# Block order for every batch, a carry-over of FFN work, earlier first transposes and fewer constants in an attention-then-FFN kernel

## The chip, the cores and the metric

The kernel runs on one core of a Trainium2 chip. The metric is device time in microseconds (us), lower is better. Executions of one kernel mostly agree within about one per cent. Now and then a run falls into a slow state; such runs are left out of every comparison.

The engines are called as in the profile: PE is TensorE (matmuls), PEld its weight loads, DVE is VectorE, ACT is ScalarE, POOL is GpSimd (here causal masks and the issuing of loads), SP issues the stores. Each engine has its own list of instructions, and one that takes long holds up those behind it on its engine.

## The reference, cut to what matters

```python
# q, k, v: (4 batches, 8 heads, 768 tokens, 64); chunks of 32 keys, 24 chunks a head
ub     = sum_d max(q * k_min[chunk], q * k_max[chunk])      # bound of each (query, chunk)
ub     = where(chunk is not in the future, ub, -1e9)
top    = the 6 chunks of largest ub, per query
scores = q @ k.T / 8, only where the key's chunk is in top and key <= query
attn   = softmax(scores) @ v
x      = attn, heads side by side                           # 3072 tokens x 512
out    = relu(x @ w_in) ** 2 @ w_out                        # 512 -> 2048 -> 512
```

## The kernel before

All matmuls are in bf16. Heads go in pairs, four pairs a batch; queries go in two blocks of 384 per batch, so there are eight query blocks. Four kinds of work share the engines.

A *preparation* of a pair transposes k and q on PE, reduces k to chunk maxima and minima on DVE, multiplies for the bounds `ub`, finds the sixth largest bound per query, and transposes the resulting selection into extra rows of q. This is a chain that goes PE, DVE, PE, DVE, ACT many times. All its results on the matmul side use one buffer, the tag `tp` of pool `pst`, so each step waits until the one before was read:

```python
pst = ctx.enter_context(tc.tile_pool(name="pst", bufs=1, space=PSUM))   # tag "tp"
psf = ctx.enter_context(tc.tile_pool(name="psf", bufs=2, space=PSUM))   # tag "ff"
...
for nm in ("k", "q"):
    pt = pst.tile([128, nt, HT, 128], BF16, tag="tp", name=nm + "T")
    ...                                              # 6 or 12 transposes by PE
    by_token = pt.rearrange("d t j p -> d t p j")
    if nm == "q":
        for hh in range(2):
            nc.scalar.copy(qs[s][hh][0:D, cols]..., by_token[...])       # ACT
        continue
    kt = work.tile([128, QB * nt], BF16, tag="kt", name="kt")
    nc.vector.tensor_copy(kt..., by_token)                               # DVE
    ...                                              # kr: max and min per chunk
```

The *attention* of a pair and a block is `ps` (scores, PE), `e` (exponential, ACT), a causal mask (POOL), `av` (values, PE), `rc` (one over the sum, ACT) and `xT` (the normalized result, DVE). A batch's first block has 3 key tiles and its second block has 6.

The *FFN* of a block can start when all four pairs of that block have written `xT`. It is cut into 28 units of four matmuls: 16 `ph` units (up) and 12 `py` units (down). A pacer puts units between the score matmuls. It drops what it could not place: the last line throws a debt away.

```python
def run_ffn(cols):
    pace["due"] += cols * pace["rate"]
    while pace["due"] >= 1.0 and ffn:
        ffn.pop(0)()
        pace["due"] -= 1.0
    pace["due"] = min(pace["due"], 1.0)
```

The *order of work*: batches 0 and 3 do their first block for all pairs and then their second (block order), batches 1 and 2 do both blocks of one pair and then the next pair (pair order). In pair order both blocks of a batch become ready for the FFN only near the batch's end.

```python
Bk = [(p, blk) for blk in range(NBLK) for p in range(NP)]
for b in range(1, B):
    heads = range(NP * b, NP * (b + 1))
    if b < B - 1:
        Bk += [(p, blk) for p in heads for blk in range(NBLK)]
    else:
        Bk += [(p, blk) for blk in range(NBLK) for p in heads]
```

At the start, 12 tiles get the same constant rows by ACT, and DVE sets the constants of all six buffer sets and two large fields of ones before its first real work.

The softmax here doesn't subtract the row's maximum and nothing guards it: scores larger than these inputs give would overflow.

## Time and profile before

The time is 357.2 us, the median of three runs (356.99 to 359.16). The profiled execution, one more run of 359.0 us, has a span of 357.3 us from its first to its last instruction. Two lines of its page, first the engines' busy times and then what all DMAs moved:

```profile
PE 308.7 (86%) x2096; PEld 160.0 (45%) x2096; DVE 218.6 (61%) x678; ACT 253.3 (71%) x589; POOL 96.7 (27%) x243
...
DMA packets 48158, 20.30 MB, mean 57 GB/s; under 512 B 41984, under 2 KB 44032, under 8 KB 48128
```

PE is the busiest engine, but an average of 86% hides different stages. The view by windows shows them. I cut the span at the last write to `xT` of batch 0's first block (48.2 us), of batch 0, 1, 2 and 3, and leave what follows as the tail. A row has the window, its length, then busy time and instructions of each engine, the granted PE clock as a share of full speed, the DMA share and GB/s:

```profile
core 0: us, PE busy (x) PEld busy (x) DVE busy (x) ACT busy (x) POOL busy (x), PEclk, DMA share, GB/s
0.00:48.20 48.20, 24.27 (x155) 11.04 (x155) 37.40 (x131) 29.04 (x60) 29.92 (x59) 1.00 1.37 172
48.20:101.90 53.70, 48.39 (x359) 25.06 (x358) 40.02 (x136) 41.52 (x102) 17.34 (x43) 0.98 0.65 68
101.90:173.20 71.30, 64.77 (x466) 34.41 (x464) 49.69 (x144) 55.87 (x135) 23.27 (x57) 0.89 0.46 49
173.20:246.70 73.50, 68.92 (x515) 36.63 (x512) 48.29 (x145) 57.75 (x136) 14.59 (x45) 1.00 0.06 23
246.70:311.50 64.80, 60.19 (x392) 31.77 (x392) 31.77 (x92) 50.14 (x123) 11.58 (x41) 1.00 0.06 21
311.50:357.30 45.80, 42.20 (x220) 21.06 (x218) 11.47 (x32) 19.01 (x38) 0.00 (x0) 0.99 0.11 41
```

The reader should see three stages: a start in which PE is busy half of the time and DVE is the fullest engine (37.4 of 48.2 us), a middle with PE nearly full, and a tail of 45.8 us that is FFN alone. The chain that ended last, read at its end (start, duration, work, count), shows the tail as matmuls nearly back to back:

```profile
310.60 0.65 PE ph L256 x4
...
311.27 10.53 PE ph L256 x60
321.80 10.36 PE py L270 x48
...
332.83 10.53 PE ph L256 x60
343.36 10.37 PE py L270 x48
```

Here four up matmuls take 0.65 us, 162 ns each, and 48 down matmuls take 10.36 us, 216 ns each. (All 64 up matmuls from 310.60 to 321.80 us average 175 ns, because a short hole follows every second unit. The prediction below divided the 10.53 us of 60 matmuls by 64 and so writes 164.) The Trainium skill, "TensorE: Matmul & The Clock Gate", section "Back-to-back issue gap", gives N/2.4 + 2.5 ns for N columns as the gap of an isolated matmul when the array is warm. This is 162.5 and 215.8 ns for 384 and 512 columns, and the trace agrees. So the tail can hardly be shortened but by having less work in it. One FFN unit of four matmuls costs about 0.77 us on average there (16 of 0.70 us and 12 of 0.86 us).

The middle has a hole that the window rows hide. The timeline of ACT, cut to the rows of the FFN (`ob` copies a finished output out, `ht` is the relu of an up result; start, duration, what), shows that in batch 1 the FFN stood still for 20 us:

```profile
140.90 0.58 ACT L275 COPY ob<-py 128x512 f32<-128x512 f32 x1
...
161.58 0.87 ACT L261 ACTIVATE ht<-ph 128x384 bf16<-128x384 f32 x2 [0.62 <-PE ph L256]
```

Both FFN blocks of batch 0 were done by 141 us, and pair order had no new block ready until 161 us. I counted FFN units per segment from the number of `ph` and `py` matmuls in each window: 1.5, 28, 39, 53, 48 and, in the tail, 55. Batch 1 has the fewest although it is as long as batch 2.

DVE's first real work, behind memsets, is this row of its timeline:

```profile
10.96 0.56 DVE L183 COPY kt<-kT 128x384 bf16<-128x384 bf16 x1
```

### The profile page before, as it was taken

The page shows a single profiled execution, that of the slowest core. Times are in us where ns is not written, and L with a number is a line of the kernel's source. Part 1 is how long each engine was busy: PE and PEld are TensorE (multiplying, and loading weights), DVE is VectorE, ACT ScalarE, POOL GpSimd, SP SyncE. Part 2 cuts the span into 40 slices and gives each one's busy share as a digit, 9 for nine tenths or more (in the row PEclk, how much of TensorE's full clock was granted, in tenths as well). Part 3 has the DMA queues.
Part 4 walks back from the last instruction along what each step waited for, and adds up shares of the span by engine and source line. Part 5 has one row for each costly group of instructions (what it writes and reads, how often), then busy time and mean ns, then how long its engine had stood idle before and what let it go on. Part 6 is the DMA issues. An engine that isn't in the chain of part 4 may idle for free.

```text
span 357.3 us, 6146 instructions
## 1 busy us (share of the span) xinstructions
PE 308.7 (86%) x2096; PEld 160.0 (45%) x2096; DVE 218.6 (61%) x678; ACT 253.3 (71%) x589; POOL 96.7 (27%) x243
## 2 busy tenths in 40 slices
PE   0276689999789998789999999999799999999996
PEld 0132345444345544445544554455444555454542
DVE  7688779747958766769482868379991331250320
ACT  6665568955968865977957897778749996671541
POOL 8275642222451332218221212212013111000000
PEclk9999999999969999959999999999999999999999
DMA  8999990190490039009400000100000000101102
GB/s 88 177 198 183 204 153 3 11 195 32 57 62 2 1 52 206 9 2 60 30 31 31 29 2 0 61 30 3 0 31 30 29 2 29 55 7 42 48 2 86
DMA packets 48158, 20.30 MB, mean 57 GB/s; under 512 B 41984, under 2 KB 44032, under 8 KB 48128
## 3 DMA queue, kind: packets, MB, share of 16 engines
q0 software_dynamic: 44672, 13.63, 36.0%
q1 hardware_dynamic: 3456, 6.29, 4.7%
q8 instruction: 16, 0.26, 0.3%
q14 instruction: 14, 0.11, 0.1%
HBM read 27.26 MB, written 6.29 MB: 94 GB/s over the span
## 4 chain that ended last, share of the span: by engine, by line
PE 57%; ACT 20%; DVE 17%; issue 4%; POOL 1%; ACTq 0%; POOLq 0%; DVEq 0%
PE ph L256 19%; PE py L270 16%; PE ps L346 7%; ACT e L350 5%; ACT rc L328 4%; ACT kqc L121 2%; ACT qsc L177 2%; PE kT L170 2%; ACT rc L331 2%; DVE qp L209 2%; DVE kr L187 2%; ACT ht L261 2%; DVE xT L334 2%; PE qT L170 2%; DVE kt L183 2%
## 5 line engine op out<-in xcount | busy, mean ns | idle before, releaser
L350 ACT ACTIVATE e<-ps 128x384 bf16<-128x384 f32 (+2 forms) x288 | 110.8, 425 | 36.8 <-PE ps L346 28.8
L256 PE MATMUL ph<-xT,w_in_sb 128*128 128x384 bf16 x512 | 108.9, 332 | 4.3 <-ACT ht L261 3.8
L353 POOL TENSOR_SCALAR_AFFINE_SELECT e<-e 128x128 bf16<-128x128 bf16 x192 | 58.7, 320 | 172.5 <-ACT e L350 171.6
L346 PE MATMUL ps<-qsc,kqc 88*128 88x384 bf16 (+2 forms) x288 | 80.7, 314 | 7.9 <-ACT e L350 4.7
L261 ACT ACTIVATE ht<-ph 128x384 bf16<-128x384 f32 x128 | 62.8, 494 | 15.9 <-PE ph L256 12.5
L256 PEld LDWEIGHTS <-w_in_sb 128*128 128x128 bf16 x512 | 49.0, 99 | 37.0 <-issue 11.2
L314 PEld LDWEIGHTS <-vo 128*128 128x128 bf16 x288 | 28.2, 103 | 29.9 <-DVE xT L334 7.5
L346 PEld LDWEIGHTS <-kqc 88*128 88x128 bf16 x288 | 28.2, 102 | 22.7 <-issue 8.3
L275 ACT COPY ob<-py 128x512 f32<-128x512 f32 x24 | 14.1, 585 | 27.5 <-PE py L270 27.5
L187 DVE TENSOR_REDUCE kr<-kt 128x24 bf16<-128x768 bf16 (+1 forms) x40 | 29.9, 786 | 0.5
L177 ACT COPY qsc<-qT 64x768 bf16<-64x768 bf16 (+1 forms) x40 | 26.6, 666 | 3.0 <-PE qT L170 2.1
L92 POOL DMA_DIRECT2D vo<-in_v_dram x24 | 21.4, 896 | 14.8 <-PE av_2351 L314 8.7
L183 DVE COPY kt<-kT 128x768 bf16<-128x768 bf16 (+1 forms) x20 | 15.9, 797 | 11.6 <-PE kT L170 11.1
L240 DVE COPY qsc<-sT 24x640 bf16<-24x640 bf16 (+2 forms) x40 | 16.7, 417 | 8.5 <-PE sT L235 8.0
L216 PE MATMUL ub<-kbd,qp 128*128 128x48 bf16 x80 | 9.8, 190 | 12.8 <-DVE qp L209 12.1
L170 PE MATMUL qT<-ident,qn 128*64 128x128 bf16 x192 | 10.8, 245 | 7.5 <-DVE kt L183 7.3
L331 ACT ACTIVATE rc<-rc 128x384 f32<-128x384 f32 x32 | 16.5, 516 | 0.2
L170 PE MATMUL kT<-ident,kn 128*64 128x128 bf16 x192 | 12.5, 247 | 4.4 <-DMA kn<-in_k_dram 4.4
L216 PEld LDWEIGHTS <-qp 128*128 128x128 bf16 x80 | 6.1, 98 | 22.3 <-DVE qp L209 22.2
L170 PEld LDWEIGHTS <-kn 128*64 128x64 bf16 x192 | 7.4, 120 | 17.7 <-issue 7.3
L211 DVE TENSOR_SCALAR qm<-qsc 64x640 bf16<-64x640 bf16 (+2 forms) x40 | 14.1, 352 | 0.0
L170 PEld LDWEIGHTS <-qn 128*64 128x64 bf16 x192 | 7.3, 120 | 14.5 <-issue 13.7
(644 smaller groups left out, 504.3 us busy)
## 6 DMA issues: line engine op xcount, KB each, us to landing
out_dram<-ob SPq DMA_DIRECT2D x24, 256.0 KB, 2.0
vo<-in_v_dram POOLq DMA_DIRECT2D x24, 128.0 KB, 4.4
kn<-in_k_dram POOLq DMA_DIRECT2D x3, 768.0 KB, 8.7
qn<-in_q_dram POOLq DMA_DIRECT2D x3, 768.0 KB, 11.3
w_in_sb<-in_moe_w_in_dram POOLq DMA_DIRECT2D x2, 1024.0 KB, 12.4
w_out_sb<-in_moe_w_out_dram POOLq DMA_DIRECT2D x2, 1024.0 KB, 12.3
kn<-in_k_dram POOLq DMA_DIRECT2D x1, 384.0 KB, 15.8
qn<-in_q_dram POOLq DMA_DIRECT2D x1, 384.0 KB, 10.1
```

Of the source, the lines that this page charges most:

```text
L170: nc.tensor.matmul(pt[D * hh:D * hh + D, t, j], lhsT=n[:, 2 * (2 * hp + hh) + n0 + t, j], rhs=ident, is_transpose=True, start=True, stop=True)
L177: nc.scalar.copy(qs[s][hh][0:D, cols].rearrange("d (t p j) -> d t p j", t=nt, j=HT), by_token[D * hh:D * hh + D])
L183: nc.vector.tensor_copy(kt.rearrange("d (t p j) -> d t p j", t=nt, j=HT), by_token)
L187: nc.vector.tensor_reduce(kr[:, m], kt.rearrange("d (c j) -> d c j", j=CH), axis=AX.X, op=op)
L256: nc.tensor.matmul(ph, lhsT=w_in_sb[:, ki, 128 * f:128 * (f + 1)], rhs=xT[:, ki, t0:t0 + QB], start=(ki == 0), stop=(ki == NKI - 1))
L261: nc.scalar.activation(ht, ph, ACT.Relu)
L270: nc.tensor.matmul(py, lhsT=h2[f][:, 128 * t:128 * (t + 1)], rhs=w_out_sb[:, f, :], start=(f == 0), stop=(f == NFI - 1))
L314: nc.tensor.matmul(hold["av"][hh][:, off:], lhsT=vo[b % 2].rearrange("p h n d -> p (h n d)")[:, c0:c0 + 2 * D], rhs=es[hh][:, off:], start ...
L331: nc.scalar.activation(rc, rc, ACT.Exp, scale=-1.0)
L346: nc.tensor.matmul(ps[:, off:], lhsT=kq[s][hh][:, 128 * j:128 * (j + 1)], rhs=qs[s][hh][:, q0 + off:q1], start=True, stop=True)
L350: nc.scalar.activation(e[:, off:], ps[:, off:], ACT.Exp, scale=scale)
L353: nc.gpsimd.affine_select(out=e[:, off:off + 128], in_=e[:, off:off + 128], compare_op=ALU.is_ge, fill=0.0, base=0, channel_multiplier=-1, ...
```

## The change

The intent is to give every stage FFN work to hide its waits, and to shorten start and tail.

1. Every batch goes in block order. Each FFN block is spread over the next query block's attention, at a rate set per block; 8 units (`KEEP`) are left over on purpose, so that the next border has something to run. The line that threw debt away is gone.
2. In batch 0's first block the transposes of k and q use the FFN's two matmul buffers (`psf`), which are idle then, and not the single `tp` buffer.
3. Of 12 constant fills on ACT one stays; 15 copies by DMA (there are now eight buffer sets) do the rest. Constants of later sets and the second field of ones are set later.
4. Batches 2 and 3 (`WIDE` is batches 0 and 1) load q and k token by token, in runs of 256 bytes instead of 768. Then the transposes come out in order: DVE needs no reordering copy `kt`, and DVE and not ACT copies q.
5. Loads are merged and placed by hand in a list of phases, and `xT` is a tile per block.

The core of the diff, with cuts marked by dots:

```diff
-    hpool = ctx.enter_context(tc.tile_pool(name="hpool", bufs=2 * NFI))
+    hpool = ctx.enter_context(tc.tile_pool(name="hpool", bufs=NFI + 8))
...
+    WIDE = (0, 1)
...
+            if b not in WIDE:
+                nc.gpsimd.dma_start(
+                    out=dst[:, h0:h1].rearrange("p h t (j d) -> p (h t j) d", d=D),
+                    in_=src[b, h0:h1].rearrange("h (j p) d -> p (h j) d", p=128))
...
-    for s in range(NSET):
         for hh in range(2):
-            nc.scalar.activation(kq[s][hh][D:KC, :]..., ident[...]..., ACT.Copy, scale=NEG)
+            if (s, hh) == (0, 0):
+                nc.scalar.activation(kq[0][0][D:KC, :]..., ident[...]..., ACT.Copy, scale=NEG)
+            else:
+                nc.sync.dma_start(out=kq[s][hh][D:KC, :], in_=kq[0][0][D:KC, :])
...
+        pool, tag = (psf, "ff") if p < NP and n1 == 1 else (pst, "tp")
         for nm in ("k", "q"):
-            pt = pst.tile([128, nt, HT, 128], BF16, tag="tp", name=nm + "T")
+            pt = pool.tile([128, nt, HT, 128], BF16, tag=tag, name=nm + "T")
...
+    KEEP = 8
...
         while pace["due"] >= 1.0 and ffn:
-            ffn.pop(0)()
+            ffn.pop(0)[1]()
             pace["due"] -= 1.0
-        pace["due"] = min(pace["due"], 1.0)
...
+    phases = []
+    for b in range(B):
+        for blk in range(NBLK):
+            phases.append([("B", NP * b + hp, blk) for hp in range(NP)])
...
+    put(0, 1, L(load_qk, 0, 0, H, (1,)), L(load_w_in))
+    put(1, 0, L(load_qk, 1, 0, H), L(load_w_out), L(load_v, 1))
+    for b in range(1, B):                       # four preparations of batch b:
+        p0 = NP * b                             # three in the block before it,
+        e = NBLK * b - 1                        # one at its own start
+        for i in range(NP - 1):
+            put(e, i + 1, ("A", p0 + i, (0, 1)))
+        put(e + 1, 0, ("A", p0 + NP - 1, (0, 1)))
+        ...
+    put(1, 2, L(nc.vector.memset, vo[1][:, :, :, D:], 1.0))
+
+    for ph, items in enumerate(phases):
+        cols = sum(768 if x[2] == 0 else 1920 for x in items if x[0] == "B")
+        pace["rate"] = (len(ffn) + nunits - KEEP) / cols if ph else 0.0
+        ...
+        while ffn and ffn[0][0] < ph - 1:
+            ffn.pop(0)[1]()
```

## The prediction

> **What bounds the kernel now.** The page has PE busy 86%, ACT 71%, DVE 61%, POOL 27% of 357.3 us. The tail runs PE back to back (chain of waits: 60 up matmuls in 10.53 us from 311.3, 48 down in 10.36 us, and both again): 164 and 216 ns each, the "N/2.4 + 2.5 ns" spacing of the Trainium skill, TensorE: Matmul & The Clock Gate, Back-to-back issue gap. With these spacings all matmuls need some 261 us (estimate: up 82, down 82, scores and values 74, preparation 23). So about 96 us are PE gaps. Cutting the span at the xT writes in the timeline: batch 0's first block ends at 48 us (gaps 38), its second at 108 (14), batch 1 at 178 (17), batch 2 at 253 (10), batch 3 at 311 (4), then 46 us of tail. DVE is busy 37 of the first 48 us; ACT starts with 12 constant fills (8.9 us, on the chain of waits); DVE's first real operation starts at 10.96 us, behind memsets, though k landed at 4.4 us.
>
> **What changes.**
> 1. Start. One ACT fill and 15 small copies by DMA replace the 12 fills: ACT -8.1 us. One of two 2.6 us memsets leaves the front; with transposes in FFN banks, q no longer waits for k. First kt copy at about 7.5 us, first exp about 15 (17.4 now), batch 0's first block done about 39 (48).
> 2. Batch 0's second block now holds six preparations. From the order of instructions and the trace's durations, DVE has about 90 us of work before it ends, so it is DVE-bound: end about 97 (108), with one more preparation done.
> 3. FFN. In block order each FFN block (28 units of 4 matmuls, 0.75 us) fills the next block, leaving 8 units over. After the last attention the PE order has 32 down, 64 up, 48 down: 36 units against about 58. Tail: about 27 + 3.6 us = 31 (46).
>    These 20-odd units aren't free: they move to where PE has gaps. Batches 1 and 2 do 56 units each (39 and 53 now), batch 3 56 (44).
> 4. Batches 2 and 3 load q and k unpermuted: DVE loses 8 kt copies (-7.7 us) but makes the q copies (+9); ACT loses 16 copies of 0.79 us (-12.7). DVE total stays near 219, ACT falls to about 232. q/k runs shrink from 768 to 256 bytes, DMA packets grow by about 16,000; DMA is nearly idle in that window, so about 0 on the path, though the skill (DMA: Bandwidth & Descriptors, Specifications) calls under 512 B inefficient.
>
> **Sum.** Second blocks: PE 39 us, ACT 37, DVE 36, so about 43; first blocks PE 28, about 30. Batches 1 and 2: 73 each (70 and 75 now), batch 3: 65 (58, with fewer units). 97 + 73 + 73 + 66 + 31 = 340 us.
>
> **Predicted: 340 us, range 331 to 350.** Chances: faster over 2% 0.89, within 2% 0.10, slower 0.01.
>
> **What would show it.** Windows: batch 0 ending 95 to 100; batch 1 and 2 about as long as now though with more FFN; batch 3 longer by 7; tail shorter by 15. Page: ACT busy about 232, DVE about 219, packets about 64,000; PE share about 91%.
>
> **What would make it wrong.** DVE in order and three engines close to their limits in the second blocks (36 to 39 of 43 us): if they wait for each other there, phases stretch and the gain halves. A late landing of w_in or v's second half (issued later, behind selects on POOL) could stall batch 0's second block. If the even mix instead hides nearly all gaps, 328.

## The result

The changed kernel took 342.6 us (median of four runs, 341.43 to 343.42) beside 357.94 us for the kernel before on the same chip. The ratio is 0.957, 95% interval 0.952 to 0.962. All ratios here are the mean time of one kernel's fast runs over that of the other kernel's fast runs of the same rounds, so they are not quite the ratios of the medians quoted. The result is correct. The profiled execution has a span of 341.6 us. Its page:

```profile
PE 298.7 (87%) x2096; PEld 158.5 (46%) x2096; DVE 222.1 (65%) x678; ACT 231.8 (68%) x562; POOL 88.5 (26%) x226
...
DMA packets 64298, 20.86 MB, mean 61 GB/s; under 512 B 58276, under 2 KB 60684, under 8 KB 64268
```

The same cut into windows, again at the last `xT` write of batch 0's first block and of each batch:

```profile
0.00:47.20 47.20, 25.10 (x158) 12.44 (x158) 40.66 (x140) 21.69 (x52) 25.79 (x54) 0.93 1.15 142
47.20:103.30 56.10, 50.66 (x407) 26.71 (x407) 47.74 (x161) 42.44 (x103) 17.05 (x38) 0.93 1.00 94
103.30:180.70 77.40, 72.05 (x560) 39.06 (x559) 57.81 (x169) 54.92 (x136) 20.71 (x50) 1.00 0.56 51
180.70:254.00 73.30, 69.94 (x520) 37.74 (x519) 49.97 (x145) 53.96 (x135) 14.63 (x50) 1.00 0.23 34
254.00:312.10 58.10, 55.12 (x326) 29.88 (x325) 20.22 (x48) 47.99 (x120) 10.30 (x36) 1.00 0.05 19
312.10:341.60 29.50, 25.83 (x132) 12.63 (x130) 5.74 (x16) 10.79 (x21) 0.00 (x0) 1.00 0.12 45
```

The tail is 29.5 us long, and its chain holds one full FFN block and 8 leftover units (32 matmuls) of the one before:

```profile
309.48 6.91 PE py L301 x32
...
317.06 10.53 PE ph L287 x60
327.59 10.38 PE py L301 x48
```

Side by side, with FFN units counted from the `ph` and `py` matmuls of each window:

| segment | before, us | units | after, us | units | difference, us |
|---|---|---|---|---|---|
| batch 0, first block | 48.2 | 1.5 | 47.2 | 1.5 | -1.0 |
| batch 0, second block | 53.7 | 28 | 56.1 | 28 | +2.4 |
| batch 1 | 71.3 | 39 | 77.4 | 56 | +6.1 |
| batch 2 | 73.5 | 53 | 73.3 | 56 | -0.2 |
| batch 3 | 64.8 | 48 | 58.1 | 50 | -6.7 |
| tail | 45.8 | 55 | 29.5 | 33 | -16.3 |
| all | 357.3 | | 341.6 | | -15.7 |

The tail lost 22 units, that is 60 up matmuls at 175 ns and 28 down at 216 ns, 16.5 us together; it became 16.3 us shorter. The question is what these 22 units cost elsewhere. The other five segments together grew by only 0.6 us, but this is net of the other parts of the change (experiment 4 puts the token-by-token loads alone at 4.5 us), so it is not the price of the units by themselves. Batch 1 took 17 of them for 6.1 us instead of the about 13 us that 17 units take in a row; they filled the hole between 141 and 161 us. Of the `ph` matmuls, before and then after, in that window (PE, ACT, PE clock, DMA share, GB/s):

```profile
140.90:161.60 20.70, 2.37 (x8) 0.02 (x1) 0.75 0.13 25
...
140.90:161.60 20.70, 11.57 (x52) 6.48 (x13) 1.00 0.01 1
```
Batch 3 took two and became 6.7 us shorter. In the kernel before, part of two preparations still lay in batch 3's first block, and of its 48 units 18.5 fell to that block (29.8 us) and 29.5 to the second (35.0 us). After the change no preparation is left in batch 3 and the units are 25 and 25 (27.0 and 31.2 us).

One caution on single segments: the granted PE clock dips for some microseconds in both profiled executions, in batch 1 before (0.89 there, and 0.75 in the window of the hole) and in batch 0 after (0.93). And the first block of one and the same program ended anywhere from 45.5 to 47.2 us in the profiles of these experiments (see experiment 12). Differences of one to three microseconds in one segment should not be read.

The start did not keep its promise. These rows of the timeline of all engines are from the changed kernel between 30 and 42 us, cut to four events (in brackets: idle time before and what ended it):

```profile
30.61 2.62 DVE L407 MEMSET vo<- 128x3072 bf16 x1 [0.70 <-issue]
33.94 0.50 PE L287 MATMUL ph<-xT,w_in_sb 128*128 128x384 bf16 x1 [1.64 <-DMA w_in_sb<-in_moe_w_in_dram]
...
39.09 2.24 POOL L102 DMA_DIRECT2D vo<-in_v_dram  x1
39.40 2.01 DVE L230 TENSOR_SCALAR qm<-qsc 64x384 bf16<-64x384 bf16 x1
```

And this is the first real work of DVE, 3.2 us earlier than the 10.96 us of before:

```profile
7.76 0.56 DVE L198 COPY kt<-kT 128x384 bf16<-128x384 bf16 x1
```

So the start began earlier, and yet the first block ended only 1 us earlier. Three things lie between: a memset of 2.62 us on DVE, a wait of 1.64 us for `w_in`, and a DVE minimum with zero (`qm`; the text of experiment 12 calls it a multiply) of 2.01 us (its kind takes 0.25 us) that ended as a long load issue on POOL ended. It held up the `xT` write behind it on DVE, which started at 41.44 us. The last experiment tests them.

### The profile page after: what moved, and what is told of

Its sections match the earlier page's. It is cut to its first block, busy times and chain, and to the rows that moved or that the text cites. A ratio compares the mean times of both kernels' runs of the same rounds, so it can differ in the third digit from the quotient of the medians.

```text
span 341.6 us, 6124 instructions
## 1 busy us (share of the span) xinstructions
PE 298.7 (87%) x2096; PEld 158.5 (46%) x2096; DVE 222.1 (65%) x678; ACT 231.8 (68%) x562; POOL 88.5 (26%) x226
## 2 busy tenths in 40 slices
DMA packets 64298, 20.86 MB, mean 61 GB/s; under 512 B 58276, under 2 KB 60684, under 8 KB 64268
## 4 chain that ended last, share of the span: by engine, by line
PE 49%; DVE 26%; ACT 14%; issue 5%; DMA 4%; POOL 1%; ACTq 0%; POOLq 0%
PE ph L287 16%; PE py L301 15%; ACT rc L358 6%; PE ps L378 5%; DVE kr L205 4%; DMA w_in_sb<-in_moe_w_in_dram 4%; DVE xT L368 4%; ACT e L382 3%; DVE kqc L212 2%; ACT rc L361 2%; DVE qm L230 2%; ACT ht L292 2%; PE kT L189 2%; PE qT L189 2%; DVE qp L229 2%
## 5 line engine op out<-in xcount | busy, mean ns | idle before, releaser
L287 PE MATMUL ph<-xT,w_in_sb 128*128 128x384 bf16 x512 | 107.5, 332 | 5.0 <-ACT ht L292 3.2
L385 POOL TENSOR_SCALAR_AFFINE_SELECT e<-e 128x128 bf16<-128x128 bf16 x192 | 56.6, 306 | 206.1 <-ACT e L382 204.4
L378 PE MATMUL ps<-qsc,kqc 88*128 88x384 bf16 (+2 forms) x288 | 75.2, 307 | 6.4 <-ACT e L382 4.1
L378 PEld LDWEIGHTS <-kqc 88*128 88x128 bf16 x288 | 27.2, 101 | 19.7 <-issue 6.4
L219 ACT COPY qsc<-qT 64x384 bf16<-64x384 bf16 (+1 forms) x24 | 14.0, 581 | 12.0 <-PE qT L189 11.6
L243 PE MATMUL ub<-kbd,qp 128*128 128x48 bf16 x80 | 8.6, 191 | 10.6 <-DVE qp L229 10.1
L205 DVE TENSOR_REDUCE kr<-kT 128x24 bf16<-128x768 bf16 x16 | 14.8, 953 | 3.4 <-PE kT L189 3.3
L361 ACT ACTIVATE rc<-rc 128x384 f32<-128x384 f32 x32 | 16.5, 516 | 0.2
L205 DVE TENSOR_REDUCE kr<-kt 128x12 bf16<-128x384 bf16 (+1 forms) x24 | 15.5, 677 | 0.2
L262 PE MATMUL sT<-ident,selb 128*128 128x128 bf16 x80 | 8.7, 236 | 4.2 <-DVE selb L255 4.0
L225 DVE COPY qsc<-qT 64x768 bf16<-64x768 bf16 x16 | 8.9, 554 | 3.4 <-PE qT L189 3.2
```

Source lines behind the costliest of these rows:

```text
L205: nc.vector.tensor_reduce(kr[:, mm], flat.rearrange("d (c j) -> d c j", j=CH), axis=AX.X, op=op)
L287: nc.tensor.matmul(ph, lhsT=w_in_sb[:, ki, 128 * f:128 * (f + 1)], rhs=xT[:, ki], start=(ki == 0), stop=(ki == NKI - 1))
L361: nc.scalar.activation(rc, rc, ACT.Exp, scale=-1.0)
L378: nc.tensor.matmul(ps[:, off:], lhsT=kq[s][hh][:, 128 * j:128 * (j + 1)], rhs=qs[s][hh][:, q0 + off:q1], start=True, stop=True)
L385: nc.gpsimd.affine_select(out=e[:, off:off + 128], in_=e[:, off:off + 128], compare_op=ALU.is_ge, fill=0.0, base=0, channel_multiplier=-1, ...
```

## The experiments

All 12 were run with five rounds against the kernel before. "After" is 342.6 us, ratio 0.957, with the segments of the table above. Where I say that batch 0 ends at some time, it is the last `xT` write of batch 0 in the profiled execution, cut as before. The theory at the outset: the gain is the even supply of FFN units, by block order together with the carry-over; the start gives a few us. Rivals: the dropped debt alone caused the long tail; the carry-over is only a cost in the tail; the constants and loads give the gain.

### 1. Before, with the debt kept

```diff
         while pace["due"] >= 1.0 and ffn:
             ffn.pop(0)()
             pace["due"] -= 1.0
-        pace["due"] = min(pace["due"], 1.0)
```

> The kernel before with one line out: FFN units that came due while none was ready are no longer forgotten. Question: did the tail fall (45.8 to 29.5 us after the last attention write) because of the order of blocks (supply of FFN work), or only because the pacing keeps its debt? Order theory: before starves in batch 1, where two FFN blocks come ready together only at its end; the debt is then paid in a burst at the start of batch 2, so the tail falls to about 31 us too but batch 2 grows by some 12 us: total 350 to 356 us, ratio to before 0.98 to 1.0. Pacing theory: nearly the whole gain, 341 to 346 us, ratio 0.955 to 0.97.

Measured: 399.8 us, ratio 1.112 (1.106 to 1.117), one of six runs slow. Neither theory held. The tail did shrink, to 26.2 us, but the batches grew to 95.3, 87.6 and 81.7 us. The PE timeline shows how:

```profile
180.31 7.01 PE L256 MATMUL ph<-xT,w_in_sb 128*128 128x384 bf16 x40
187.25 10.52 PE L270 MATMUL py<-w_out_sb,h 128*128 128x512 bf16 x47
```

With pair order there are stretches with no unit to run, such as the 20 us above. There the debt grows, and when blocks come the whole FFN block runs in a row, 17 us without attention; after that attention runs alone again. So the dropped debt was a sound guard in the kernel before. The granted clock was lower too, 0.927 over this profiled run and 0.85 to 0.86 in batch 1, so not all of the 42 us need be the bursts; but batch 3, at 0.97 to 0.99, still took 81.7 us (64.8). A shorter tail is worth nothing by itself: what counts is whether the units meet attention to overlap with.

### 2. After, nothing carried over

```diff
-    KEEP = 8
+    KEEP = 0
```

> The kernel after without the carry-over of 8 FFN units. Theory: the carry-over only fills the start of a block while the last heads of the block before are still unfinished; without it the tail is 8 units (6 us) shorter and each of 6 block borders loses up to 1 to 2 us of TensorE work: total 339 to 346 us against 342, tail about 23.5 us. Rival: the carry-over does not matter, TensorE is anyhow the limit: 336 us.

Measured: 357.3 us, ratio 0.998 (0.995 to 1.002). The whole gain is gone. The tail is 4.6 us shorter (24.9), but the first blocks of batches 1, 2 and 3 take 34.9, 33.8 and 32.7 us (29.8, 26.9 and 27.0), and the last block 37.1 (31.2). The PE timeline at the border from batch 1 to batch 2:

```profile
186.34 8.66 PE L287 MATMUL ph<-xT,w_in_sb 128*128 128x384 bf16 x49
194.85 3.61 PE L301 MATMUL py<-w_out_sb,h 128*128 128x512 bf16 x15
```

With nothing left over, the units of the block that has just ended come in one burst, 12 us without a score matmul, and ACT has no exponentials to do. With 8 leftover units both kinds of work go on across the border, and the loss is gone. The prediction had seen this line only as a cost in the tail. But two lines act together here. The code can pay such a burst only because the change also took out the line that limits the debt to one unit; `KEEP = 0` with that line back was not run. So what is shown is that a carry-over is needed once the debt is kept, not that it would be needed in any pacer.

### 3. After, 16 carried over

```diff
-    KEEP = 8
+    KEEP = 16
```

> The kernel after with 16 units carried over instead of 8. Taking the carry-over away cost 14.8 us (run e2), because TensorE then ran 64 up and 15 down matmuls in one burst at the border while ScalarE had only ht to do, and attention alone later. With 8 a burst of 36 up matmuls is still in TensorE's order at each such border; with 16 there is none. Theory (even mix is what counts): the first blocks of batches 2 and 3 (26.9 us each) and the blocks after fall together by 2 to 6 us, the tail grows by up to 6 us: total 338 to 344. Rival (8 already covers the border): the tail's 6 us are lost, about 346 to 349.

Measured: 349.8 us (median of the five fast runs; 350.3 with the slow one), fast ratio 0.976 (0.974 to 0.979). The profiled execution fell in the slow state, so no time is read from its trace. It is 7.2 us slower than 8. The number of matmuls doesn't depend on the state: 70 up and 96 down lie in the tail of that trace, 41.5 units and not 33. At 0.77 us each (an estimate) 8.5 more units cost 6.5 us, most of the loss. So it seems that the value for the borders is had by 8 units, and that what is above is paid in the tail; no fast trace shows the borders with 16.

### 4. After, all batches loaded as batches 0 and 1

```diff
-    WIDE = (0, 1)
+    WIDE = (0, 1, 2, 3)
```

> The kernel after with batches 2 and 3 loaded permuted in 768-byte runs as in before (the copies of q back on ScalarE, the kt copy back on VectorE). Prediction's theory: about 0 on the path, within 1.5 us of after (341 to 344 us); ScalarE busy 12.7 us more, VectorE about 1 less, packets 16,000 fewer. Rival: ScalarE and TensorE are close to balance in the second blocks, so 12.7 us of ScalarE work comes back as 4 to 8 us of time in batches 1 and 2.

Measured: 347.1 us, ratio 0.969 (0.966 to 0.972), 4.5 us more than after. ACT's busy time is back up, from 231.8 to 242.5:

```profile
PE 300.9 (87%) x2078; PEld 158.4 (46%) x2096; DVE 216.8 (63%) x686; ACT 242.5 (70%) x578; POOL 84.9 (25%) x226
```

The second blocks of batches 1 and 2, where the preparations of batches 2 and 3 lie, take 49.6 and 49.2 us (47.6 and 46.3). Batch 0 ended 3.6 us earlier (99.7), with no long issue of token-by-token loads in its second block; 1.5 us of that lie in the first block, which this edit doesn't touch (see experiment 12). So the token-by-token loads are worth 4.5 us in all, in the second blocks and in spite of a price in batch 0. That it is the work taken off ACT is likely but not shown apart: the edit also brings back the `kt` copy as a step of each preparation.

### 5. After, the constants filled by ACT again

```diff
-            if (s, hh) == (0, 0):
+            if True:
                 nc.scalar.activation(
-                    kq[0][0][D:KC, :]...
+                    kq[s][hh][D:KC, :]...
```

> The kernel after with the constant rows of the keys filled by ScalarE again (16 fills of 0.84 us, spread, instead of one and 15 copies by DMA). Prediction's theory: the fills were on the chain, so they cost 3 to 8 us again, 346 to 350. Rival: VectorE (40.7 of the first 47.2 us busy) bounds the start and ScalarE has room there (21.7 us busy): within 1.5 us of after.

Measured: 343.9 us, ratio 0.959 (0.957 to 0.961), 1.3 us more than after, and the first block ended at 48.3 us. The intervals overlap, so even 1.3 us is not settled. The fills put about 10 us back on ACT, but ACT has room in that stage: 32.8 us busy of the first 48.3. Eight of the 16 fills ran before 10.6 us and the others spread over the block, so this isn't quite the 12 in a row of before; but the 8.9 us of fills on the chain of waits before were hardly 8 us to be won.

### 6. After, the first transposes in the single buffer again

```diff
-        pool, tag = (psf, "ff") if p < NP and n1 == 1 else (pst, "tp")
+        pool, tag = (pst, "tp")
```

> The kernel after with the first transposes back in the single bank that all preparation shares. Prediction's theory: q then waits for k's copies again (6.7 us of waiting at the start of before), so the first block ends 3 us later and the total grows by up to 3 us: 344 to 346. Rival: VectorE has the same work either way and sets the pace of the first block; within 1.5 us of after.

Measured: 351.3 us, ratio 0.980 (0.978 to 0.983), 8.7 us more than after. All of it lies in batch 0 (first block ends at 59.1 us); later segments are equal. The first four preparations follow each other at about 6.5 us, and in the changed kernel at 4 to 5.5 us. But the order of DVE's work moved too. The big memset now lay in the middle of the first preparation, and PE waited for the selection behind it. A row of DVE's timeline, then one of PE's:

```profile
13.84 2.62 DVE L407 MEMSET vo<- 128x3072 bf16 x1 [0.59 <-issue]
...
17.10 0.39 PE L262 MATMUL sT<-ident,selb 128*128 128x128 bf16 x2 [4.65 <-DVE selb L255]
```

So the 8.7 us are the two FFN buffers and a worse place of a memset together. No run splits them, but the trace gives a hint: the first selection (`selb`) came 2.8 us later than in after (16.79 and 14.01), where the memset lies, and the fourth 9.0 us later (37.55 and 28.53), so about 6 us built up behind the memset.

### 7. After, loads spread over batch 0's second block

```diff
-    put(1, 0, L(load_qk, 1, 0, H), L(load_w_out), L(load_v, 1))
+    put(0, 3, L(load_w_out))
+    put(1, 0, L(load_qk, 1, 0, H))
+    put(1, 1, L(load_v, 1))
```

> The kernel after with the four DMA issues at the start of batch 0's second block (k, q of batch 1, w_out, v of batch 1; 5.7 us in a row on GpSimd from 35.7 us) spread: w_out one head pair earlier, v one later. Theory: VectorE is shut out by GpSimd while it writes descriptors (qm took 0.95 and 2.01 us for two instructions there against 0.25), which held the xT write until 41.4 us and left ScalarE waiting 4.4 us: first block ends at about 44 us (47.2) and the total falls by 2 to 4 us, to about 339. Rival: VectorE's own 40.7 us of work in the first 47.2 us is the limit, and the total stays within 1 us.

Measured: 343.7 us, ratio 0.960 (0.957 to 0.964). No gain. The first block ended later (52.4), since one more half preparation (its selection written from 49.8 us on) came before its last `xT` write, and batch 0 ended at 103.0 as before.

### 8. After, with the debt dropped again

```diff
             ffn.pop(0)[1]()
             pace["due"] -= 1.0
+        pace["due"] = min(pace["due"], 1.0)
```

> The kernel after with the line of before that forgets FFN units that came due while none was ready. Theory: debt makes bursts, and each block's rate takes up what was left over, so dropping it gives the same or less: 339 to 344, tail unchanged (TensorE's order ends alike: 32 down, 64 up, 48 down). Rival: the debt is needed to keep the FFN up with the blocks: 347 or more.

Measured: 344.5 us, ratio 0.962 (0.959 to 0.964), at most 1.9 us more than after. The intervals overlap. The line that was worth 42 us in the kernel before matters little here. A likely reason is that with block order and a carry-over the pacer is seldom without units; this was not counted.

### 9. After, two of batch 1's preparations later

```diff
-        for i in range(NP - 1):
-            put(e, i + 1, ("A", p0 + i, (0, 1)))
-        put(e + 1, 0, ("A", p0 + NP - 1, (0, 1)))
+        now = 1 if b == 1 else NP - 1
+        for i in range(now):
+            put(e, i + 1 if b > 1 else NP - 1, ("A", p0 + i, (0, 1)))
+        for i in range(now, NP):
+            put(e + 1, max(i - 1, 0) if b == 1 else 0, ("A", p0 + i, (0, 1)))
```

> The kernel after with two of the three preparations of batch 1 moved out of batch 0's second block into the first block of batch 1. Theory: VectorE bounds batch 0 (88.4 of 103.3 us busy; the last head pair of the second block takes 19 us there, behind two whole preparations of 8.3 us in VectorE's order), so batch 0 ends at 90 to 95 us instead of 103; the next block has VectorE busy 17 of 29.8 us and can take it with 5 to 8 us more: total 335 to 341. Rival (something else, such as the cold TensorE clock or the late weights, bounds it): 342 to 345.

Measured: 343.7 us, ratio 0.959 (0.957 to 0.961). No change that the noise lets one see. Batch 0 still ended at 102.3 us, though one whole preparation fewer (48 transposes of k in the second block and not 60) lay before that. If DVE's amount of work set the end of batch 0, as the prediction said, this should have ended it several us earlier.

### 10. After, the reordering copy of k on ACT

```diff
-                    nc.vector.tensor_copy(
+                    nc.scalar.copy(
                         kt.rearrange("d (t p j) -> d t p j", t=nt, j=HT),
                         by_token)
```

> The kernel after with the eleven permuting copies of kT (batches 0 and 1; 0.56 or 0.96 us each, 8.3 us in all) on ScalarE instead of VectorE. Moving preparations to a later block (run e9) changed nothing; this takes work off VectorE. Theory (each preparation is one chain through VectorE, about 9 us long, and paces batch 0): batch 0 ends 3 to 6 us earlier, total 337 to 341, VectorE busy 214. Rival (ScalarE is as much on the chain): within 1.5 us, ScalarE busy 240.

Measured: 350.5 us, ratio 0.979 (0.976 to 0.983), 8 us more than after. DVE's busy time fell from 222.1 to 215.0 us and ACT's rose to 237.2. Batch 0's second block took 64.0 us (56.1), and DVE waited for ACT at the head of the preparations:

```profile
87.91 1.81 DVE L205 TENSOR_REDUCE kr<-kt 128x24 bf16<-128x768 bf16 x2 [1.96 <-ACT kt L198]
...
97.60 1.81 DVE L205 TENSOR_REDUCE kr<-kt 128x24 bf16<-128x768 bf16 x2 [1.45 <-ACT kt L198]
```

With experiment 9 this speaks against DVE's throughput as the limit of batch 0: an engine that is short of throughput should gain from having work taken away. It is no clean test, since the copy was not removed but given to ACT. What the rows show is DVE waiting for ACT at this hand-over, 1.96 and 1.45 us.

### 11. After, batches 2 and 3 never loaded (wrong on purpose)

```diff
             dst = nat[nm, b]
+            if b > 1:
+                continue
             if b not in WIDE:
...
+        if b > 1:
+            return
         if half is None:
```

(Batches 2 and 3 use the tiles of batches 0 and 1 again.)

> Wrong result on purpose: the kernel after without the loads of batches 2 and 3 (they reuse the data of 0 and 1), so that six of its nine large DMA issues and 36,864 short packets are gone. Theory (GpSimd writing descriptors shuts VectorE out: a kqc copy took 1.98 us instead of 0.26 beside the issue of q for batch 2 at 76.7 us, with TensorE busy 1.7 of 4 us there): batch 0 ends at about 100 us and the total falls by 2 to 5 us. Rival (the loads are hidden, as the prediction said): within 1 us of after. Either way the whole price of these loads is measured.

Measured: 340.4 us, ratio 0.950 (0.947 to 0.953), with a wrong result as intended. Only 2.3 us are gone, and in the profile they lie in batch 0's second block (53.7 us, 56.1 in after). The later segments didn't change by more than 0.4 us each. So the DMA work of batches 2 and 3 costs at most that. It lies where batch 2's q and k are issued, two issues of 2.23 us each on POOL from 74.5 us on; that the issue and not the transfer is the price was not tested apart.

### 12. After, with three stalls of the start mended

```diff
-    put(0, 1, L(load_qk, 0, 0, H, (1,)), L(load_w_in))
+    put(0, 1, L(load_w_in), L(load_qk, 0, 0, H, (1,)))
...
-    put(1, 0, L(load_qk, 1, 0, H), L(load_w_out), L(load_v, 1))
+    put(1, 0, L(load_qk, 1, 0, H), L(load_w_out))
+    put(1, 1, L(load_v, 1))
...
-    put(1, 2, L(nc.vector.memset, vo[1][:, :, :, D:], 1.0))
+    put(0, 0, L(nc.scalar.copy, vo[1][:, :, :, D:], vo[0][:, :, :, D:]))
```

> The changed kernel with three stalls of its start mended: the ones of vo's second buffer are copied by ScalarE at the start and not set by VectorE at 30.6 us (2.62 us), w_in is issued before the second halves of batch 0's k and q (TensorE waited 1.64 us for it), and batch 1's long v load is issued one head pair later than its k, q and w_out (its 2.24 us on GpSimd stood beside a VectorE multiply of 2.01 us, .25 us alone). Theory: the head start of the FFN banks was eaten by these stalls between 28 and 42 us, and batch 0 keeps what is mended: first block ends at about 41 to 43 us instead of 47.2, total 336 to 340 us. Rival: the chain across VectorE, ScalarE and TensorE of the later preparations swallows it, as it swallowed two earlier edits of the order: first block may end earlier, but batch 0 ends at 101 to 104 us, total 341 to 344 us.

Measured: 340.8 us (six runs, 339.83 to 342.19), ratio 0.953 (0.949 to 0.956); correct. Its median is the lowest of all correct versions, but its interval overlaps that of after (0.952 to 0.962), so its lead of 1.8 us is not settled. The first block ended at 44.8 us (47.2), later than the theory's 41 to 43, and batch 0 at 101.2 us (103.3), at the rival's lower edge. The total lies just above the theory's range and just below the rival's. The mended stalls are gone, but only 2.4 us of about 6 arrived. Where two went is in the trace. These are rows of the timeline of all engines:

```profile
32.37 0.56 DVE L198 COPY kt<-kT 128x384 bf16<-128x384 bf16 x1 [2.44 <-PE kT L189]
...
35.79 0.17 DVE L210 COPY kbd<-kr 64x24 bf16<-64x24 bf16 x1
...
45.73 2.23 POOL L102 DMA_DIRECT2D vo<-in_v_dram  x1
45.91 2.02 DVE L210 COPY kbd<-kr 64x24 bf16<-64x24 bf16 x2
```

Where the memset had been, DVE now stood idle for 2.44 us until PE had the next `kT` ready. In after these transposes began at the same time (31.3 us), so of the memset's 2.62 us some 1.8 had only filled this wait. The v load moved to 45.73 us, and the stall moved with it, to another operation: now two small copies, 0.17 us each elsewhere, take 2.02 us and end, at 47.93, where the issue ends, at 47.96. In after it was the minimum `qm` that ended at 41.41 when the issue ended at 41.33. So a long issue on POOL does hold DVE up, wherever it is put. The Trainium skill, "SBUF — State Buffer", section "Who interferes with whom", states that VectorE and GpSimd share a pair of ports under an exclusive lock, which copies and operations with a scalar of VectorE can need and its reductions do not. The trace agrees: beside a third issue of the changed kernel (74.48 to 76.71 us) two reductions took their usual 1.00 us together.

In experiments 2, 4, 8 and 9 the first block is the same program as in after, but in their profiles POOL's issues ran 0.5 to 0.7 us later, and the `qm` that took 2.01 us in after slipped in as the issue of v began. This is its row in experiment 9:

```profile
39.67 0.24 DVE L230 TENSOR_SCALAR qm<-qsc 64x384 bf16<-64x384 bf16 x1
```

In these four the first block ended at 45.5 to 45.8 us; in experiment 11, where the issues ran as in after and `qm` took 2.00 us, it ended at 47.2. So this stall is worth about 1.5 us, it comes and goes from one profile to the next, and the mended kernel's 44.8 us are only 0.7 to 1.0 us better than a run without it.

## Why the prediction was right or wrong

The total was right, 340 predicted and 342.6 measured, and so was the direction. It was right partly because errors cancelled. The predicted sum was 97 + 73 + 73 + 66 + 31; measured are 103.3 + 77.4 + 73.3 + 58.1 + 29.5.

- **Tail: right.** Predicted 31 us with 36 units against about 58, measured 29.5 us with 33 against 55. The unit counts and the times in the trace gave this term.
- **Moved units fill gaps: right, and shown.** Batch 1 was predicted to do 56 units instead of 39 and did; they landed in a stretch where FFN had stood still (141 to 161 us). Experiments 1 and 2 show that a short tail alone wins nothing: the units must not come in bursts.
- **"Batch 0's first block done about 39 (48)": wrong by 8 us.** Its pieces were partly right. The first `kt` copy came at 7.76 us (predicted 7.5) and the first exponential at 16.1 (predicted about 15). Experiment 6 puts the separate buffers, with the better place of the memset, at 8.7 us. What failed is the step from an earlier start to an earlier end. The first block inherited a memset, a wait for `w_in` and a blocked DVE, with DVE busy 40.7 of the 47.2 us. Experiment 12 mends the three and ends it 2.4 us earlier, of which about 1.5 us is the blocked DVE alone; some 1.8 us of the memset had filled a wait for `kT`. What holds the rest of the 8 us wasn't found.
- **"ACT -8.1 us" from the constants: wrong as a saving in time.** Experiment 5 gives 1.3 us. They were on the chain of waits, but DVE's memsets ran beside them until 10.93 us.
- **"So it is DVE-bound: end about 97 (108)": wrong twice.** The old end was miscounted by one pair; it is 101.9 in the windows (the old ends of batches 1 and 2 were miscounted likewise). And giving DVE's copy to ACT (experiment 10) or moving preparations out (experiment 9) did not speed this stage. It ended 1.4 us later than before, at 103.3.
- **Batch 1, 73 predicted, 77.4 measured:** the units were right; the stage overlapped them a little less well. **Batch 3, 66 predicted, 58.1 measured:** I counted 56 units there, but 50 lie there. Six units at 0.77 us are about 4.6 of the 8 us. The other 3.3 us were not tested by a run of their own.
- **"About 0 on the path" for the loads of batches 2 and 3: wrong.** Experiment 4 gives 4.5 us in their favour, in the second blocks and likely by ACT's relief; experiment 11 shows a price of about 2 us, in batch 0. The prediction looked for cost in the DMA engines. The Trainium skill, "DMA: Bandwidth & Descriptors", section "Specifications", wants transfers of at least 512 bytes for full rate. Packets under 512 bytes rose from 41,984 to 58,276 here, and no later stage became longer by it.
- **The carry-over: missing.** The prediction counted its 8 units as a cost. Experiment 2 shows that without them, with the debt kept, the whole gain of about 15 us is gone.
- **Busy times:** ACT 232 predicted, 231.8 measured; DVE 219 and 222.1; packets 64,000 and 64,298; PE's share 91% and 87%. The last was too high because PE's own busy time fell by 10 us as well.

Two things stay open. Block order was never run alone: no experiment gives the kernel before block order and nothing else, or the changed kernel pair order, so the gain of the order isn't separated from that of the carry-over and the new pacing. And it is open what exactly paces batch 0. Experiments 7, 9 and 10 each tried one cause and failed; experiment 12 won about 2 us in the first block. The remaining account, a chain from engine to engine in which each step waits for what another engine has before it, fits all four, but no run isolates it.

## What to carry to other kernels

When two kinds of work are mixed to hide each other's waits, count the units that each stretch of time really has, and look for stretches that run dry: the 17 units moved into batch 1 take about 13 us by themselves and made it only 6.1 us longer (net of the other edits), while forcing work out in bursts (experiment 1) made the kernel 11% slower. Keep a small backlog across borders; here, with the debt kept, 8 units of 28 were the best of three, 0 lost the whole gain and 16 lost nearly half of it. And time won at the head of a chain is only a claim until the end of that stage moves: look for the long load issues and waits that sit on an engine between the two, and ask of each whether something else would have been waited for in its place.

## What the Trainium skill lacked or had wrong

- "SBUF — State Buffer", section "SBUF: two separate sides": its warning describes VectorE holding up the descriptor writing of a DMA that GpSimd issues. The lock rule of the page covers the other direction too, but for a slowed VectorE the page has only a bare factor ("DVE 6.8× slower", section "Who interferes with whom") and no case beside the issue of a load. Here it is the direction that costs: a `qm` minimum took 2.01 us for about 0.25 beside an issue of 2.24 us, and two copies of 0.17 us took 2.02 us beside an issue of 2.23 us (experiment 12). Both ended within 0.1 us of the issue.
- None of the pages that I read gives the time of an issue by GpSimd by its number of contiguous runs. Here 6,144 runs of 256 bytes (a batch of v) kept POOL for 2.23 us and 2,048 runs of 768 bytes (a batch of k) for about 1.16 us.
- "TensorE: Matmul & The Clock Gate", section "Back-to-back issue gap": the formula agrees (162 and 216 ns measured, over 4 and 48 matmuls). But the section calls it the gap of an isolated matmul and says that a stream of weight loads and matmuls sustains about 131 ns at 512 columns; here 48 down matmuls in such a stream took 216 ns each. Over the whole changed kernel PE was busy 298.7 us for an estimated 261 us of matmuls at that spacing.
